# Two transformer layers on one core: three heads per attention slot, unpadded K, static tiles and hand-ordered streams

## Chip, core and metric

The kernel runs on one core of one Trainium2 chip. A core has a matrix engine (TensorE, PE in the profile, with its weight loads as PEld), a vector engine (DVE), a scalar engine that evaluates the exponential (ACT), GpSimd (POOL) and SyncE (SP), which here only issues transfers. Each engine works through its own queue in order; semaphores tie the queues together. Matmuls write to PSUM, a memory of eight banks of 512 fp32 columns on 128 partitions; ACT and DVE read from it.

The metric is device time in microseconds (us) of one execution. PEclk in the profile is the share of full TensorE speed that the clock throttle granted.

## What is computed

Two times the same pair of blocks: multi-head attention on the layer-normed x, added to x, then a ReLU MLP on the layer-normed x, added to x. Both layers use the same weights. S = 2048 tokens, D = 512, 32 heads of width 16, hidden width 1792; inputs and outputs are bfloat16.

```python
    def _A_ref(x, wqkv, wo):
        ...
        qkv = (lambda x, *d: x.transpose(*d))((x @ wqkv).reshape(B, S, 3, H, Dh), 2, 0, 3, 1, 4)
        q, k, v = qkv[0], qkv[1], qkv[2]
        scores = jnp.einsum("bhqd,bhkd->bhqk", q, k) * (Dh ** -0.5)
        p = _softmax(scores, axis=-1)
        o = jnp.einsum("bhqk,bhkd->bhqd", p, v)
        return (lambda x, *d: x.transpose(*d))(o, 0, 2, 1, 3).reshape(B, S, D) @ wo
    def _B_ref(x, w1, w2):
        h = jnp.einsum("bsd,df->bsf", x, w1)
        ...
        h = jnp.maximum(h, zero)
        return jnp.einsum("bsf,fd->bsd", h, w2)
    x = A_x
    x = x + _A_ref(_layernorm(x, axis=-1), A_wqkv, A_wo)
    x = x + _B_ref(_layernorm(x, axis=-1), B_w1, B_w2)
    x = x + _A_ref(_layernorm(x, axis=-1), A_wqkv, A_wo)
    x = x + _B_ref(_layernorm(x, axis=-1), B_w1, B_w2)
```

## The kernel before

**Tiling.** Tokens are cut into 16 tiles of 128 (for keys, for x and for the MLP) and 4 chunks of 512 queries. Heads go in 8 sets of four; head g of a set sits at partitions 32g to 32g + 15 of the padded Q and K (`wq_pad`, `wk_pad`, lines 81 to 97; half of each padded projection is zeros). One (chunk, set) pair is called a unit here: 32 units per layer, each over 16 key blocks.

**One key block of a unit.** `s_pair` (line 288, matmul at 293) computes transposed scores, 128 keys by 512 queries, of two heads into two banks, the heads on separate 32-row strips of the array. `e_pair` (301, the exponential at 303) takes the exponential of both at once, 128 x 1024, into SBUF. `pv_pair` (306, matmul at 310) multiplies by V, which carries a column of ones ahead of each head's 16 columns, so that row 0 of each head's strip of `pso` sums the exponentials. The pairs A and B (heads 0, 1 and 2, 3) take turns, each with two PSUM banks; `pso` has three buffers of one bank, cleared by DVE beforehand (319); the eighth bank, `ovl`, serves all other matmuls.

**Normalization** (`norm_item`, 322): copy of `pso`, a matmul with `esel` that spreads each sum over its strip (326), a copy (328), a reciprocal of 128 x 512 (329), a product (330).

**Filler work.** Q of the unit after next (`qchunk`, 204), output projection (`outproj_items`, 332), layer norms (`ln_stats_rstd` at 141 with a reciprocal square root by 13 Newton steps on DVE; `ln_apply` at 169 with four PE transposes a tile) and the MLP in halves of 256 tokens (`mlp_chunk_items`, 215) stand in two lists, `urgent` and `work`; `drain(1)` takes one entry after each key block. All their matmul groups share the `ovl` bank while attention runs. A scheduler of the tile framework settles the order on each engine's queue from the program order and priorities, so PE's order in the trace differs in places from the text.

**Stages.** Load and pad weights, layer norm of all 16 tiles, V for all, K for all (`vproj_all` 192, `kproj_all` 181); attention of layer one with the MLP of each finished chunk as filler; the remaining work with four PSUM buffers; V and K of layer two; attention of layer two; remaining work; stores.

**Queues of transfers.** SP: 16 loads of x, at the end 16 stores. POOL: wqkv. ACT: 32 small loads of `wo` rows (72), w1 and w2 (77, 79).

Of the kernel before, what the change touches and what calls it, by code (L numbers as in the profile page):

```python
# [10 lines left out]
BF16 = mybir.dt.bfloat16  # L11
ACTF = mybir.ActivationFunctionType
ALU = mybir.AluOpType

EPS = 1e-5


@with_exitstack
def kernel(
# [16 lines left out]
    H = 32  # L36
# [15 lines left out]
    identity_pool = ctx.enter_context(tc.tile_pool(name="identity_pool", bufs=1))  # L52

    ident = identity_pool.tile([P, P], BF16, name="ident")
    make_identity(nc, ident[:])

    x_tiles = []
    for tt in range(NTT):
        xt = persist.tile([P, D], BF16, name=f"x{tt}")
        nc.sync.dma_start(out=xt[:], in_=x_flat[tt * P : (tt + 1) * P, :])  # L60
        x_tiles.append(xt)

    wst_pool = tc.alloc_tile_pool(name="wst_pool", bufs=1)
    wqkv_st = wst_pool.tile([P, NDC, 3 * D], BF16, name="wqkv_st")
    nc.gpsimd.dma_start(out=wqkv_st[:], in_=A_wqkv[:, :].rearrange("(c p) f -> p c f", p=P))
    wo_pad = []
    for t in range(NT):
        wo_t = persist.tile([P, D], BF16, name=f"wo_pad{t}")
        nc.gpsimd.memset(wo_t[:], 0.0)
        for g in range(4):  # L70
            h = 4 * t + g
# [3 lines left out]
        wo_pad.append(wo_t)  # L75
    w1 = persist.tile([P, NDC, DFF], BF16, name="w1")
    nc.scalar.dma_start(out=w1[:], in_=B_w1[:, :].rearrange("(c p) f -> p c f", p=P))
    w2 = persist.tile([P, NF, D], BF16, name="w2")
    nc.scalar.dma_start(out=w2[:], in_=B_w2[:, :].rearrange("(c p) f -> p c f", p=P))

    wq_pad = []
    wk_pad = []
    for t in range(NT):
        wq_t = persist.tile([P, NDC, P], BF16, name=f"wq_pad{t}")
        wk_t = persist.tile([P, NDC, P], BF16, name=f"wk_pad{t}")
        nc.gpsimd.memset(wq_t[:], 0.0)
        nc.gpsimd.memset(wk_t[:], 0.0)
        for g in range(4):
# [43 lines left out]
    def gps():  # L132
        return cur_ps[0]
# [314 lines left out]
```

## Time and profile before

| | us |
|---|---|
| median of 3 runs | 2723.09 |
| lowest, highest run | 2709.48, 2730.97 |
| span of the profiled execution, first to last instruction | 2728.0 |
| PE busy | 2593.9 |
| ACT busy | 2049.6 |
| DVE busy | 840.6 |
| ACT idle before exponentials, waiting for scores | 447.9 |
| ACT idle before its table load, at the start | 106.0 |

The profile is of one execution; for that execution the span is the time there is, and it lies within the three runs, 4.9 us above their median. Busy time of an engine is the union of its instructions. A busy PE isn't PE at its best: at half clock the same matmul is busy for longer. A row of instructions reads: line, engine, operation, written tile <- read tiles, shapes, count, then busy time, mean ns of one, idle time of the engine just before them and what ended it. A timeline row reads: start, duration of the merged run of instructions, engine, line, operation, count. A matmul's modelled duration includes about 0.17 us in which the next one already streams.

### The profile page before, as it was taken

How to read it: one execution, taken by the hardware profiler on the slowest of the kernel's cores; microseconds unless marked ns; L12 is line 12 of the kernel's file. 1: busy time of each engine (PE TensorE's matmuls, PEld its weight loads, DVE VectorE, ACT ScalarE, POOL GpSimd, SP SyncE). 2: the span in 40 equal slices, each digit the busy share in tenths (PEclk: the TensorE clock that was granted, in tenths of full speed). 3: DMA queues.
4: the chain of work that ended last, by engine and by line, in shares of the span. 5: the costliest groups of instructions: out<-in, count | busy, mean ns of one | idle time of the engine just before them, and what ended most of it. 6: DMA issues, size and time to landing. Idle time of an engine off the chain costs nothing.

```text
span 2728.0 us, 27669 instructions
## 1 busy us (share of the span) xinstructions
PE 2593.9 (95%) x10752; PEld 645.9 (24%) x10752; DVE 840.6 (31%) x1842; ACT 2049.6 (75%) x2049; POOL 16.1 (1%) x52
## 2 busy tenths in 40 slices
PE   2999999999999999999859999999999999999996
PEld 1311112321222212232133111123212321123213
DVE  7411113321323214331274111143213331243215
ACT  0488886898758987589604888868987798869990
POOL 2000000000000000000000000000000000000000
PEclk9855556975558756595578555569755895569757
DMA  3000000000000000000000000000000000000000
GB/s 116 1 1 1 1 0 1 1 1 1 1 0 1 1 1 1 1 1 1 0 1 1 1 1 1 0 0 5 5 1 1 3 7 1 1 1 5 4 1 8
DMA packets 8371, 11.73 MB, mean 4 GB/s; under 512 B 1072, under 2 KB 7472, under 8 KB 8240
## 3 DMA queue, kind: packets, MB, share of 16 engines
q1 hardware_dynamic: 4608, 4.20, 0.5%
q10 hardware_dynamic: 3360, 4.20, 0.5%
q8 instruction: 84, 1.38, 0.2%
q0 software_dynamic: 272, 1.57, 0.1%
q14 instruction: 47, 0.39, 0.0%
HBM read 7.86 MB, written 2.10 MB: 4 GB/s over the span
## 4 chain that ended last, share of the span: by engine, by line
PE 85%; ACT 6%; DVE 6%; issue 2%; DMA 1%; ACTq 0%; SPq 0%
PE pss L293 33%; PE pso L310 32%; ACT expt L303 6%; PE ph L229 5%; PE pz L247 4%; PE poz L343 3%; PE pq L207 3%; PE pk L186 2%; PE pt L178 1%; PE pv L196 1%; PE pb L326 1%; DVE rs_t L162 1%; DVE rs_y L166 1%; DVE rs_t L160 1%; DVE rs_t L161 1%
## 5 line engine op out<-in xcount | busy, mean ns | idle before, releaser
L303 ACT ACTIVATE expt<-pss 128x1024 bf16<-128x1024 f32 x2048 | 2048.3, 1026 | 505.2 <-PE pss L293 447.9
L293 PE MATMUL pss<-qch,ktp 32*128 32x512 bf16 x4096 | 1140.9, 531 | 23.9 <-ACT expt L303 21.2
L310 PE MATMUL pso<-expt,vaug 128*17 128x512 bf16 x4096 | 1120.8, 527 | 0.9 <-ACT expt L303 0.9
L293 PEld LDWEIGHTS <-ktp 32*128 32x128 bf16 x4096 | 222.5, 96 | 834.2 <-issue 826.2
L310 PEld LDWEIGHTS <-vaug 128*17 128x17 bf16 x4096 | 194.3, 89 | 757.0 <-issue 747.1
L324 DVE CAST u<-pso 128x512 bf16<-128x512 f32 x64 | 44.1, 690 | 1048.1 <-PE pso L310 1048.1
L329 DVE RECIPROCAL pbs<-pbs 128x512 f32<-128x512 f32 x64 | 214.5, 3352 | 2.1
L229 PE MATMUL ph<-xn2T,w 128*128 128x256 bf16 x896 | 158.8, 302 | 0.9
L233 DVE TENSOR_SCALAR ht<-ph 128x256 bf16<-128x256 f32 x224 | 93.1, 418 | 210.3 <-PE ph L229 209.9
L178 PE MATMUL pt<-ident,xn 128*128 128x128 bf16 x256 | 56.9, 287 | 92.1 <-DVE xn L171 91.3
L247 PE MATMUL pz<-w,ht 128*128 128x512 bf16 x448 | 118.9, 382 | 0.6
L343 PE MATMUL poz<-wo_pad,ot 128*128 128x512 bf16 x256 | 103.1, 525 | 9.0 <-DVE x L348 4.7
L207 PE MATMUL pq<-xnT,wq_pad 128*128 128x512 bf16 x256 | 110.5, 511 | 1.2 <-DVE x L348 0.8
L229 PEld LDWEIGHTS <-w 128*128 128x128 bf16 x896 | 75.8, 105 | 74.8 <-issue 63.7
L303 ACT ACT_TABLE_LOAD x1 | 1.3, 1283 | 106.0 <-DVE qch L212 106.0
L212 DVE CAST qch<-pq 128x512 bf16<-128x512 f32 x64 | 44.1, 691 | 112.6 <-PE pq L207 111.8
L252 DVE TENSOR_TENSOR x<-x,pz 128x512 bf16<-128x512 bf16 x32 | 22.0, 687 | 147.6 <-PE pz L247 147.2
L348 DVE TENSOR_TENSOR x<-x,poz 128x512 bf16<-128x512 bf16 x32 | 22.0, 687 | 134.7 <-PE poz L343 134.7
L178 PEld LDWEIGHTS <-xn 128*128 128x128 bf16 x256 | 25.6, 112 | 156.6 <-DVE xn L171 100.2
L328 DVE COPY pbs<-pb 128x512 f32<-128x512 f32 x64 | 44.2, 691 | 40.6 <-PE pb L326 40.6
L186 PE MATMUL pk<-xnT,wk_pad 128*128 128x512 bf16 x256 | 55.6, 379 | 0.0
L179 DVE COPY xn2T<-pt 128x128 bf16<-128x128 bf16 x128 | 26.3, 222 | 91.1 <-PE pt L178 90.8
(41 smaller groups left out, 558.6 us busy)
## 6 DMA issues: line engine op xcount, KB each, us to landing
w<-in_B_w_dram ACTq DMA_DIRECT2D x2, 1792.0 KB, 10.9
x<-in_A_x_dram SPq DMA_DIRECT2D x16, 128.0 KB, 7.9
out_dram<-x SPq DMA_DIRECT2D x16, 128.0 KB, 1.7
wqkv_st<-in_A_wqkv_dram POOLq DMA_DIRECT2D x1, 1536.0 KB, 11.7
wo_pad<-in_A_wo_dram ACTq DMA_DIRECT2D x32, 16.0 KB, 1.7
```

The costliest lines, as they stand in the source:

```text
L178: nc.tensor.transpose(pt[:], xn[:, c * P : (c + 1) * P], ident[:])
L186: nc.tensor.matmul(pk[:], wk_pad[t][:, c, :], xnT[c][:, 512 * j : 512 * (j + 1)], start=(c == 0), stop=(c == NDC - 1),)
L207: nc.tensor.matmul(pq[:], wq_pad[t][:, c, :], xnT[c][:, qs * QS : (qs + 1) * QS], start=(c == 0), stop=(c == NDC - 1),)
L229: nc.tensor.matmul(ph[:], w1[:, c, ft * P : (ft + 1) * P], xn2T[c][:, c0 : c0 + HW], start=(c == 0), stop=(c == NDC - 1),)
L233: nc.vector.tensor_scalar(out=ht_half[ft][:], in0=ph[:], scalar1=0.0, scalar2=None, op0=ALU.max)
L247: nc.tensor.matmul(pz[:], ht_half[ft][:, ttl * P : (ttl + 1) * P], w2[:, ft, :], start=(ft == 0), stop=(ft == NF - 1),)
L293: nc.tensor.matmul(pss[:, QS * gi : QS * (gi + 1)], ktp[32 * g : 32 * g + 32, kb * P : (kb + 1) * P], qch[32 * g : 32 * g + 32, :], start= ...
L303: nc.scalar.activation(out=expt[:], in_=pss[:], func=ACTF.Exp, scale=SCALE)
L310: nc.tensor.matmul(pso[32 * g : 32 * g + VAW, :], vaug[kb][:, h, :], expt[:, QS * gi : QS * (gi + 1)], start=(kb == 0), stop=(kb == NKB - ...
L328: nc.vector.tensor_copy(out=pbs[:], in_=pb[:])
L329: nc.vector.reciprocal(out=pbs[:], in_=pbs[:])
L343: nc.tensor.matmul(pz[:], ot_all[t][:, ttl * P : (ttl + 1) * P], wo_pad[t][:], start=(t == 0), stop=(t == NT - 1),)
```

## The change

The function is rewritten. What it does, part by part:

- **Blocks and slots.** The unit of scheduling is a block (unit, key block, head). Three consecutive blocks form a slot: three score matmuls into one of two three-bank buffers `ps_s`, one exponential of 128 x 1536, and two slots later three value matmuls. Slots run on across key blocks and units; 2048 blocks of a layer make 683 slots. Four buffers hold exponentials.
- **PSUM.** Six banks for scores, one for the value sums (`ps_o`), one for filler work (`ps_f`). When attention isn't running (`wide`), filler work goes round seven banks.
- **Layouts.** K isn't padded: the projection's 128 columns hold eight heads of 16, four of them (even or odd) used per unit, and only Q's weights are padded with zeros, so that a contraction over a 32-row strip picks one head. There are 4 instead of 8 K projections per 512 tokens. V of head pairs is laid out with two columns of ones between them; a value matmul takes 32 columns, so the sum stands in row 16 or 15 of the strip. No clearing of the sums, no `esel` matmul.
- **Normalization.** Copy of `ps_o`, a stream shuffle on DVE that spreads the sum over its 32 partitions, the reciprocal in four parts of 128 columns, a product; after the copy, one such DVE instruction is issued per slot.
- **Reciprocal square root.** Bit-shift seed and 4 Newton steps of three instructions, per four tiles, where it was 13 steps of four.
- **Order.** The scheduler is off (`manual_schedule`): each engine runs in program order. All other work consists of pieces, mostly two matmuls each. `run_until` forces pieces that a slot needs; `run_some` paces the rest over the remaining slots of the chunk.
- **Start.** Layer norm, K and V of chunk 0 come first, then Q and the first slots; K and V of chunks 1 to 3 are made within the first unit, ahead of the key blocks that need them. K and V of layer two are made chunk by chunk as filler in layer one.
- **MLP** in chunks of 512 tokens instead of halves of 256.
- **Transfers.** On SP: four tiles of x, K's weights, the other tiles, 32 loads of `wo` rows, w1, w2; each output tile is stored when it is done. On ACT's queue: Q's and V's weights. Q's padded weights are built by POOL.

```diff
-    NT = H // 4
-    VAW = DH + 1
...
-    for t in range(NT):
-        wo_t = persist.tile([P, D], BF16, name=f"wo_pad{t}")
...
-            nc.scalar.dma_start(
-                out=wo_t[32 * g + 1 : 32 * g + 1 + DH, :], in_=A_wo[DH * h : DH * h + DH, :]
-            )
...
-    def ln_stats_rstd(tts):
...
-    def ln_apply(tt, xnT_dst, col0):
...
-    def kproj_all(xnT):
...
-    def vproj_all(xnT):
...
-    def mlp_chunk_items(qs, xnT_next, do_ln1next, work):
...
-    def mha_layer(xnT_cur, xnT_next, do_ln1next):
...
+    NT = 8
+    PW = 34
+    W = 3
+    NE = 4
+    ctx.enter_context(tc.manual_schedule())
...
+    ktp = [
+        [[sb([P, QS], BF16, f"ktp{l}_{T}_{j}") for j in range(NQS)] for T in range(4)]
+        for l in range(2)
+    ]
+    vaug = [[sb([P, H // 2, PW], BF16, f"vaug{l}_{kb}") for kb in range(NKB)] for l in range(2)]
+    ebuf = [sb([P, W, QS], BF16, f"e{n}") for n in range(NE)]
+    qbuf = [sb([P, QS], BF16, f"q{n}") for n in range(3)]
+    ubuf = [sb([P, QS], FP32, f"u{n}") for n in range(2)]
+    ps_s = [psum.tile([P, W, QS], FP32, name=f"ps_s{n}") for n in range(2)]
+    ps_o = psum.tile([P, QS], FP32, name="ps_o")
+    ps_f = psum.tile([P, QS], FP32, name="ps_f")
...
+    for tt in range(4):
+        nc.sync.dma_start(out=x_t[tt][:], in_=x_flat[tt * P : (tt + 1) * P, :])
+    nc.scalar.dma_start(out=wqkv[:, :, 0:D], in_=wq_src[:, :, 0:D])
+    nc.sync.dma_start(out=wqkv[:, :, D : 2 * D], in_=wq_src[:, :, D : 2 * D])
+    nc.scalar.dma_start(out=wqkv[:, :, 2 * D : 3 * D], in_=wq_src[:, :, 2 * D : 3 * D])
+    for tt in range(4, NTT):
+        nc.sync.dma_start(out=x_t[tt][:], in_=x_flat[tt * P : (tt + 1) * P, :])
...
+    for t in range(NT):
+        nc.gpsimd.memset(wq_pad[t][:], 0.0)
+    for kb in range(NKB):
+        nc.gpsimd.memset(vaug[0][kb][:, :, DH : DH + 2], 1.0)
+    for t in range(NT):
+        T, e = divmod(t, 2)
+        nc.gpsimd.tensor_copy(
+            out=wq_pad[t][:].rearrange("p c (g e d) -> p c g e d", g=4, e=2)[:, :, :, e, :],
+            in_=wqkv[:, :, T * P : (T + 1) * P].rearrange(
+                "p c (g e d) -> p c g e d", g=4, e=2
+            )[:, :, :, e, :],
+        )
+    for t in range(NT):
+        nc.gpsimd.memset(wo_pad[t][:], 0.0)
+        T, e = divmod(t, 2)
+        for g in range(4):
+            h = 8 * T + 2 * g + e
+            r0 = 32 * g + 16 * e
+            nc.sync.dma_start(out=wo_pad[t][r0 : r0 + DH, :], in_=A_wo[DH * h : DH * h + DH, :])
+    nc.sync.dma_start(out=w1[:], in_=B_w1[:, :].rearrange("(c p) f -> p c f", p=P))
+    nc.sync.dma_start(out=w2[:], in_=B_w2[:, :].rearrange("(c p) f -> p c f", p=P))
+    for kb in range(NKB - TPC):
+        nc.gpsimd.memset(vaug[1][kb][:, :, DH : DH + 2], 1.0)
+    def bank():
+        if not wide[0]:
+            return ps_f[:]
+        n = bank_no[0] % 7
+        bank_no[0] += 1
+        if n == 6:
+            return ps_f[:]
+        return ps_s[n // W][:, n % W, :]
+    def run_some(budget):
+        while budget > 0:
+            piece = next_piece()
+            if piece is None:
+                return
+            piece[1]()
+            budget -= piece[0]
+    def run_until(key):
+        while key not in done:
+            piece = next_piece()
+            assert piece is not None, key
+            piece[1]()
+    def ln_stats(j):
+        n = ln_no[0] % 2
+        ln_no[0] += 1
+        for i in range(TPC):
+            st = stats[i % 2]
+            nc.vector.bn_stats(out=st[:], in_=x_t[j * TPC + i][:])
+            nc.vector.bn_aggr(out=mv[n][:, i, :], in_=st[:])
+        a, y, t1 = va_[n], ya_[n], ta_[n]
+        nc.vector.tensor_scalar(
+            out=a[:], in0=mv[n][:, :, 1], scalar1=EPS, scalar2=None, op0=ALU.add
+        )
+        nc.vector.tensor_scalar(
+            out=t1[:].bitcast(I32), in0=a[:].bitcast(I32), scalar1=1, scalar2=None,
+            op0=ALU.logical_shift_right,
+        )
+        nc.vector.tensor_scalar(
+            out=y[:].bitcast(I32), in0=t1[:].bitcast(I32), scalar1=-1.0,
+            scalar2=float(RSQRT_SEED), op0=ALU.mult, op1=ALU.add,
+        )
+        for _ in range(4):
+            nc.vector.scalar_tensor_tensor(
+                out=t1[:], in0=y[:], scalar=-0.5, in1=y[:], op0=ALU.mult, op1=ALU.mult
+            )
+            nc.vector.tensor_mul(out=t1[:], in0=t1[:], in1=a[:])
+            nc.vector.scalar_tensor_tensor(
+                out=y[:], in0=t1[:], scalar=1.5, in1=y[:], op0=ALU.add, op1=ALU.mult
+            )
+        return n
+    def ln_groups(j, dst, key):
+        hold = {}
+        groups = []
+        def st():
+            hold["n"] = ln_stats(j)
+        for i in range(TPC):
+            def piece(i=i):
+                if i == 0:
+                    st()
+                n = hold["n"]
+                xn = xnbuf[i % 3]
+                nc.vector.tensor_scalar(
+                    out=xn[:], in0=x_t[j * TPC + i][:],
+                    scalar1=mv[n][:, i, 0:1], scalar2=ya_[n][:, i : i + 1],
+                    op0=ALU.subtract, op1=ALU.mult,
+                )
+                pt = bank().bitcast(BF16)
+                for c in range(NDC):
+                    nc.tensor.transpose(
+                        pt[:, c * P : (c + 1) * P], xn[:, c * P : (c + 1) * P], ident[:]
+                    )
+                nc.vector.tensor_copy(
+                    out=dst[:, :, i * P : (i + 1) * P],
+                    in_=pt[:, 0 : NDC * P].rearrange("p (c f) -> p c f", c=NDC),
+                )
+                if i == TPC - 1:
+                    done.add(key)
+            groups.append([(1.3, piece)])
+        return groups
+    def mm_group(mms, fin, per=2):
+        hold = {}
+        pieces = []
+        n = len(mms)
+        for a in range(0, n, per):
+            def piece(a=a):
+                if a == 0:
+                    hold["b"] = bank()
+                b = hold["b"]
+                for i in range(a, min(a + per, n)):
+                    lhsT, rhs = mms[i]
+                    nc.tensor.matmul(b, lhsT, rhs, start=(i == 0), stop=(i == n - 1))
+                if a + per >= n:
+                    fin(b)
+            pieces.append((min(per, n - a), piece))
+        return pieces
+    def k_group(l, T, j):
+        def fin(b):
+            nc.vector.tensor_copy(out=ktp[l][T][j][:], in_=b)
+            done.add(("k", l, T, j))
+        return mm_group(
+            [(wqkv[:, c, D + T * P : D + (T + 1) * P], xnT[j][:, c, :]) for c in range(NDC)], fin
+        )
...
+    def q_group(n, t, j):
+        def fin(b):
+            nc.vector.tensor_copy(out=qbuf[n % 3][:], in_=b)
+            done.add(("q", n))
+        return mm_group([(wq_pad[t][:, c, :], xnT[j][:, c, :]) for c in range(NDC)], fin)
+    def rest_of_chunk(l, j):
+        gs = [o_group(j, i) for i in range(TPC)]
+        gs += ln_groups(j, xn2T[:], ("ln2", l, j))
+        gs += [h_group(ft) for ft in range(NF)]
+        gs += [z_group(l, j, i) for i in range(TPC)]
+        if l == 0:
+            gs += before_attention(1, j)
+        return gs
+    def before_attention(l, j):
+        gs = ln_groups(j, xnT[j][:], ("ln", l, j))
+        gs.append(k_group(l, 0, j))
+        gs += [v_group(l, kb) for kb in range(j * TPC, (j + 1) * TPC)]
+        gs += [k_group(l, T, j) for T in range(1, 4)]
+        return gs
...
+    def norm_items(n, t):
+        u, r = ubuf[n % 2], rbuf[n % 2]
+        e = t % 2
+        lane = DH if e == 0 else DH - 1
+        def copy():
+            nc.vector.tensor_copy(out=u[:], in_=ps_o[:])
+        def shuf():
+            nc.vector.stream_shuffle(out=r[:], in_=u[:], mask=[lane] * 32)
+        def recip(a):
+            nc.vector.reciprocal(out=r[:, a : a + P], in_=r[:, a : a + P])
+        def mul():
+            nc.vector.tensor_mul(out=ot[t][:], in0=u[:], in1=r[:])
+        return copy, [shuf] + [lambda a=a: recip(a) for a in range(0, QS, P)] + [mul]
+    def emit_pv():
+        if not pend:
+            return
+        slot = pend[0]
+        n0 = slot["blocks"][0][0]
+        while slot["blocks"] and slot["blocks"][0][0] == n0:
+            n, kb, g, w = slot["blocks"].popleft()
+            l, j, t = units[n]
+            T, e = divmod(t, 2)
+            nc.tensor.matmul(
+                ps_o[32 * g : 32 * g + 32, :],
+                vaug[l][kb][:, 4 * T + g, 2 * e : 2 * e + 32],
+                slot["e"][:, w, :],
+                start=(kb == 0), stop=(kb == NKB - 1),
+                tile_position=(0, 32 * g), skip_group_check=True,
+            )
+            if kb == NKB - 1 and g == 3:
+                copy, rest = norm_items(n, t)
+                copy()
+                dve_q.extend(rest)
+                if t == NT - 1:
+                    dve_q.append(lambda l=l, j=j: work.extend(rest_of_chunk(l, j)))
+        if not slot["blocks"]:
+            pend.popleft()
...
+    def attention(l):
+        nonlocal slot_no
+        first = l * NQS * NT
+        blocks = deque(
+            (n, kb, g)
+            for n in range(first, first + NQS * NT)
+            for kb in range(NKB)
+            for g in range(4)
+        )
+        total = len(blocks) // (NQS * NT)
+        per_chunk = NT * NKB * 4 / W
+        while blocks:
+            now = [blocks.popleft() for _ in range(min(W, len(blocks)))]
+            for n, kb, g in now:
+                _, j, t = units[n]
+                if kb == 0 and g == 0:
+                    if n == first:
+                        urgent.append(q_group(n, t, j))
+                    if n + 1 < first + NQS * NT:
+                        _, jn, tn = units[n + 1]
+                        urgent.append(q_group(n + 1, tn, jn))
+                run_until(("q", n))
+                run_until(("k", l, t // 2, kb // TPC))
+            wide[0] = False
+            b = ps_s[slot_no % 2]
+            e = ebuf[slot_no % NE]
+            for w, (n, kb, g) in enumerate(now):
+                _, j, t = units[n]
+                kt = ktp[l][t // 2][kb // TPC]
+                kc = (kb % TPC) * P
+                nc.tensor.matmul(
+                    b[:, w, :],
+                    kt[32 * g : 32 * g + 32, kc : kc + P],
+                    qbuf[n % 3][32 * g : 32 * g + 32, :],
+                    start=True, stop=True, tile_position=(32 * g, 0),
+                )
+            m = len(now)
+            ex = nc.scalar.activation(
+                out=e[:, :m, :], in_=b[:, :m, :], func=ACTF.Exp, scale=SCALE
+            )
+            if last_exp[slot_no % NE] is not None:
+                tc.declare_no_dep(
+                    ex.ins, last_exp[slot_no % NE],
+                    reason="the matmuls that read the buffer between the two writes order them",
+                )
+            last_exp[slot_no % NE] = ex.ins
+            for n, kb, g in now:
+                run_until(("v", l, kb))
+            drain_pv(1)
+            pend.append(
+                {"e": e, "blocks": deque((n, kb, g, w) for w, (n, kb, g) in enumerate(now))}
+            )
+            if dve_q:
+                dve_q.popleft()()
+            slot_no += 1
+            rest = len(blocks) / W % per_chunk
+            todo = left(urgent) + left(work) + sum(c for c, _ in cur)
+            run_some(max(todo / max(rest - 6.0, 4.0), 0.01) if todo else 0)
+        drain_pv(0)
+        wide[0] = True
+        while dve_q:
+            dve_q.popleft()()
+        run_all()
...
+    for g in before_attention(0, 0):
+        urgent.append(g)
+    for j in range(1, NQS):
+        work.extend(before_attention(0, j))
+    attention(0)
+    attention(1)
```

`rest_of_chunk` calls `o_group`, `h_group` and `z_group`, which are `mm_group`s of 8, 4 and 14 matmuls whose last step on DVE adds to x, applies the ReLU, or adds to x and, in layer two, stores the tile. `v_group` is one of 4 matmuls per key block.

More of the change, by code (lines that the diff above doesn't have):

```diff
@@ L15 @@
 EPS = 1e-5
+RSQRT_SEED = 0x5F3759DF
 @with_exitstack
@@ new lines, in run_some, with run_all @@
+    def run_some(budget):
[10 more added lines that the diff above has]
+            piece[1]()
+    def run_all():
+        while True:
+            piece = next_piece()
+            if piece is None:
+                return
+            piece[1]()
```

396 lines of the change are left out of this document (88 added, 308 removed).

## The prediction

> **What bounds the kernel now.** I read the page's span and engine rows first, then the clock row, then the busy time by stretch, cut at the first and last exponential of each layer.
>
> ```profile
> span 2728.0 us, 27669 instructions
> PE 2593.9 (95%) x10752; PEld 645.9 (24%) x10752; DVE 840.6 (31%) x1842; ACT 2049.6 (75%) x2049; POOL 16.1 (1%) x52
> ACT  0488886898758987589604888868987798869990
> PEclk9855556975558756595578555569755895569757
> ...
> 0.00:107.33 107.33, 57.46 (x276) 27.12 (x276) 81.04 (x288) 1.28 (x1) 16.07 (x52) 1.00 0.22 74
> 107.33:1344.53 1237.20, 1224.38 (x4915) 278.08 (x4914) 322.90 (x606) 1025.71 (x1024) 0.00 (x0) 0.63 0.00 1
> 1344.53:1472.12 127.59, 92.22 (x459) 46.54 (x459) 94.81 (x282) 0.00 (x1) 0.00 (x0) 0.82 0.00 1
> 1472.12:2660.83 1188.71, 1175.33 (x4885) 270.63 (x4885) 302.85 (x543) 1022.60 (x1024) 0.00 (x0) 0.66 0.01 2
> 2660.83:2728.00 67.17, 44.54 (x219) 23.49 (x218) 38.99 (x124) 0.00 (x1) 0.00 (x0) 0.72 0.03 8
> ...
> 300.00:400.00 100.00, 100.00 (x368) 18.30 (x366) 13.52 (x13) 90.85 (x89) 0.00 (x0) 0.50 0.00 1
> 500.00:600.00 100.00, 97.55 (x519) 28.43 (x517) 34.99 (x47) 92.27 (x97) 0.00 (x0) 0.93 0.00 1
> ```
>
> A stretch row is: its time, then busy time and count of PE, weight loads, DVE, ACT, POOL, the granted clock, DMA. Three stretches have no exponential: 107 us of head, 128 between the layers, 67 of tail. The other 2426 us are attention, with PE at 99%, yet not at its best: between 300 and 400 PE is busy all the time at half clock. There only 368 − 4 x 89 = 12 matmuls are full-array ones; the others fill a quarter each. From 500 to 600, 519 − 4 x 97 = 131 full-array matmuls are mixed in and the clock is 0.93. So the granted clock follows how much of the array is filled, and the stretches without filler work are bound by a slow PE, those with it by ACT or by both in turn. The Trainium skill, "TensorE: Matmul & The Clock Gate", Part 1, has the full clock granted after some 3.4 us of sustained PE activity. If busy time is meant, the 300 to 400 row disagrees, 100% busy at 0.50; what the rule would make of the sum is rival D.
>
> Now the pitches inside attention.
>
> ```profile
> 251.21 0.61 PE L293 MATMUL pss<-qch,ktp 32*128 32x512 bf16 x2
> 251.75 0.60 PE L310 MATMUL pso<-expt,vaug 128*17 128x512 bf16 x2
> ...
> 493.31 0.39 PE L310 MATMUL pso<-expt,vaug 128*17 128x512 bf16 x3
> 493.63 0.39 PE L293 MATMUL pss<-qch,ktp 32*128 32x512 bf16 x2
> ...
> 496.11 1.04 PE L207 MATMUL pq<-xnT,wq_pad 128*128 128x512 bf16 x4
> 497.07 0.39 PE L310 MATMUL pso<-expt,vaug 128*17 128x512 bf16 x2
> ...
> 499.15 5.61 ACT L303 ACTIVATE expt<-pss 128x1024 bf16<-128x1024 f32 x6 [0.24 <-PE pss L293]
> ...
> L303 ACT ACTIVATE expt<-pss 128x1024 bf16<-128x1024 f32 x2048 | 2048.3, 1026 | 505.2 <-PE pss L293 447.9
> ```
>
> A pair of score matmuls, or of value matmuls, runs side by side and takes 0.54 us to the next group at half clock (251.21 to 251.75) and 0.32 at full (493.31 to 493.63). In that row three value matmuls, not two, fit in one 0.39 us group: a third tile rides along free. Four full matmuls take 0.96 us at full clock (496.11 to 497.07), of which 3 x 0.217 = 0.65 is between their starts (1.04 − 0.39); so one streams for 0.217 us, about twice that at half clock, and a change of shape costs about 0.10. Six exponentials take 5.61 us, one 1.026, so the pitch is (5.61 − 1.026)/5 = 0.917 us.
>
> **The change part by part.**
>
> *Slots of three.* 2 x 2048 blocks (32 units x 16 key blocks x 4 heads per layer) go in 683 slots per layer, 1366 in all, where there were 2048 exponentials. The price of a 1536-wide exponential isn't in the trace. Upper end: no fixed part, 1.5 x 0.917 = 1.376 us. For the fixed part the nearest rows are DVE evacuations of 512 and 256 columns:
>
> ```profile
> L329 DVE RECIPROCAL pbs<-pbs 128x512 f32<-128x512 f32 x64 | 214.5, 3352 | 2.1
> L233 DVE TENSOR_SCALAR ht<-ph 128x256 bf16<-128x256 f32 x224 | 93.1, 418 | 210.3 <-PE ph L229 209.9
> L190 DVE CAST ktp<-pk 128x512 bf16<-128x512 f32 x64 | 44.2, 691 | 11.0 <-PE pk L186 11.0
> L146 DVE BATCH_NORM_STATS2 stats<-x 128x6 f32<-128x512 bf16 x64 | 43.8, 687 | 1.7
> L330 DVE TENSOR_TENSOR ot<-u,pbs 128x512 bf16<-128x512 bf16 x64 | 43.7, 683 | 0.6
> L319 DVE MEMSET pso<- 128x512 f32 x64 | 31.0, 485 | 10.4 <-DVE u L324 8.9
> L171 DVE TENSOR_SCALAR xn<-x,mv_all,rstd_all 128x512 bf16<-128x512 bf16 x64 | 24.0, 406 | 0.4
> L162 DVE TENSOR_SCALAR rs_t<-rs_t 128x4 f32<-128x4 f32 (+2 forms) x130 | 22.1, 170 | 4.3
> ```
>
> 0.691 − 0.418 for 256 columns leaves 0.145 fixed. Taken over to ACT: (1.026 − 0.145) x 1.5 + 0.145 − (1.026 − 0.917) = 1.358. Twice that fixed part would give 1.285. I take 1.358, between the two: 1366 x 1.358 = 1855 us (1755 to 1880). The Trainium skill, "ScalarE: Activation LUTs", What ACT_TABLE_LOAD costs, gives 186 ns + 0.833 ns a column with 93 ns overlapped: an estimate of 1.372 a slot, which would make the sum below 19 us longer; for 1024 columns it says 1.039 for one alone, where the trace has 1.026.
>
> *PE beside it.* A slot needs one trio of score and one of value matmuls. Side by side as above: 0.64 us at full clock, 1.07 at half. Both are below 1.358, so plain attention is ACT-bound even at half clock. The pacing adds one piece of two full matmuls a slot while there is work: 2 x 0.217 + 0.10 = 0.53, together 1.17 at full clock; at half clock 1.07 + 0.87 + 0.10 = 2.03, too much. Work per chunk of layer 0, in pieces: 16 output projection, 4 layer norm, 28 hidden, 28 second MLP, 4 norm and 16 K/V for the next layer, 16 Q: 112 slots; of layer 1: 92. So 3 x 112 + 3 x 92 = 612 paced slots of 1366. Per 100 us they hold 100/1.358 x 2 = 147 full matmuls, more than the 131 of the 500 row: the clock should be full there, and half in the rest, where it does no harm.
>
> *The single filler bank.* A group's first matmul waits until DVE has emptied the one bank.
>
> ```profile
> 1352.30 0.39 PE L343 MATMUL poz<-wo_pad,ot 128*128 128x512 bf16 x1 [1.82 <-DVE ot L330]
> 1352.73 0.69 DVE L348 TENSOR_TENSOR x<-x,poz 128x512 bf16<-128x512 bf16 x1 [0.48 <-PE poz L343]
> 1353.47 3.33 PE L343 MATMUL poz<-wo_pad,ot 128*128 128x512 bf16 x8 [0.78 <-DVE x L348]
> ```
>
> From that matmul's end of streaming (1352.30 + 0.217) to the next is 0.95 us; the trios between cover 0.75. So 0.2 is exposed in at most every second slot: (1.17 + 1.37)/2 = 1.27, still under 1.358. I cost it at nothing; the cover is 0.09 a slot, and if it is gone see rival B.
>
> *Layer norm in the stream.* The first piece of a norm puts its transposes on PE's queue behind all DVE statistics: 4 x (0.687 + about 0.17 for its small follow-up) + 15 x 0.170 + 0.406 = 6.4 us, plus the 0.95 for the addition before, less 0.75 for the trios: PE, and the score trio queued behind, stand 6.6 us. ACT has about one slot in hand, so 5.6 us are lost, 9 times (6 in layer 0, 3 in layer 1): 50. The three later pieces each wait for their 0.406 us normalization behind a 0.69 copy: about 0.4 over, 27 times: 11. After such a hole the clock falls and some three slots run at 2.03: 2 us x 9 = 18. The chip's 13 Newton steps become 4; the old steps cost more, but the wait stays.
>
> *Unit ends.* The value sums have one bank instead of three, so the next unit's trio waits 0.95 for the copy. A slot has about 0.5 in hand: 0.45 x 64 = 29 us. A Q group alone in a plain stretch: two slots at 2.03, less the slack, 0.8 us; 36 units are plain (7 + 9 in layer 0, 8 + 12 in layer 1): 29.
>
> *Removed or moved at no cost.* The broadcast matmul, its copy and the 0.485 us clearing of each sum go; a shuffle takes their place (unseen; I take 0.69 by the copy row) and the reciprocal is cut in four, 0.84 each, one a slot. DVE has by these rows 64 x 6.1 for the norms, about 330 for the rest: a third of the span, not a bound. K without padding halves 256 matmuls and 64 copies. On SP, 4 + 12 loads of x with K's weights between, then 32 small loads and w1 and w2:
>
> ```profile
> 0.74 15.47 SPq L60 DMA_DIRECT2D x<-in_A_x_dram  x16
> x<-in_A_x_dram SPq DMA_DIRECT2D x16, 128.0 KB, 7.9
> out_dram<-x SPq DMA_DIRECT2D x16, 128.0 KB, 1.7
> w<-in_B_w_dram ACTq DMA_DIRECT2D x2, 1792.0 KB, 10.9
> ```
>
> At about 1 us an issue the last is out near 52 us and landed by 75; the MLP first needs it after 250. If SP ran four times slower, chunk 1 would wait. On POOL the padded K weights go and eight copies that build Q's come in, unseen there (between a 0.17 us small operation and a 0.69 us copy of DVE). POOL's whole old program is 16.07 us busy in the head row, and the first Q is due only near 25: nothing, or 10 more on the head if POOL were twice as slow.
>
> *Head, joint, tail.* Head: four x tiles at about 9, statistics 4, normalizing and transposing 4.5, 36 matmuls (K, V, Q of one chunk) about 12, two evacuations 1.9, table 1.3 (the one ACT instruction in the head row): 33 us for 107. In the first unit three more chunks are forced in ahead of their keys, each about 9 us: 27. Joint: last values 0.8, normalization 0.25 + 0.69 + 0.69 + 3.35 + 0.68 with waits 6.6, 32 projections (cold at first) 10, norm 11.4, 56 hidden matmuls 14.5, 56 second ones 12 + 1, norm 11.4, K/V 10, Q 2, first scores 0.6: 80 for 128. Tail: the same up to the second MLP product and 3 for the store (0.97 to issue by SP's row, 1.7 to land): 60 for 67.
>
> Sum: 33 + 27 + 1855 + 50 + 11 + 18 + 29 + 29 + 80 + 60 = 2192. The sum is made against the span of 2728.0, 4.9 above the median of the runs, 2723.09; I take those 5 off: 2187.
>
> **The rivals.** A, as summed: ACT sets the pace. Its own range is 2090 (exponential at its low end) to 2290 (stalls doubled).
>
> B: the filler bank and in-order waits set the paced slots at 1.7 us instead of 1.358 (PE trails, and each evacuation shows whole: 1.17 + 0.95/2 = 1.65). 612 x 0.34 = 208: 2395. For it: the 0.78 waits above. Against: the trios between groups.
>
> C: the clock stays at half while paced: 612 x (2.03 − 1.358) = 411, less the 18: 2580. For it: 300 to 400. Against: 500 to 600.
>
> D: the clock stays full all through, since three tiles fill three quarters where two filled half: 18 and 29 go, 2140. The 300 row speaks against, as far as two tiles go. By the clock rule of the Trainium skill cited above the time would be this one too.
>
> E, slower: score trios don't run as three; the third tile queues. It costs 0.217 a trio at full clock and 0.43 at half. Plain slots become 2 x (0.54 + 0.43) = 1.93 and paced ones 2 x (0.32 + 0.217) + 0.53 = 1.60: 754 x 1.93 + 612 x 1.60 = 2434, and with the other 337 us of the sum about 2770, up to 3570 where paced slots run at half clock too (1.93 + 0.87 + 0.10 = 2.90). It decides from a mean slot of (2728 − 337)/1366 = 1.75 us. Against: the row with x3; no row shows three score tiles.
>
> **How the numbers follow.** A 0.56, B 0.20, D 0.10, C 0.08, E 0.06. Likeliest 2187. Low to high 2090 to 2400 holds A, D and B, 0.86. Faster by over 1% (what a measurement here can tell from none) are A to D, 0.94; E is split 0.05 slower, 0.01 the same.
>
> **What would show it.** Right: exponentials 1.34 to 1.38 apart over long stretches; clock full where MLP matmuls run and half elsewhere; nine holes of about 6 us ended by the normalized tile; gaps of 33, 80 and 60 us without exponentials. Wrong: trios over 0.45 us at full clock (E), PE over 95% busy in paced stretches with ACT waiting for scores (B at a high clock, C at a low one).

## Result, and the profile after

The changed kernel takes 2257.75 us (median; 2256.56 to 2260.01), against 2722.32 for the kernel before in the same comparison: a ratio of 0.8334, 95% interval 0.8272 to 0.8396. The forecast was 2187, the range 2090 to 2400.

The page of the changed kernel (span, busy times, the 40 slices of ACT and clock), then its busy time by stretch, cut at the first and last exponential of each layer and after the first unit:

```profile
span 2255.5 us, 23128 instructions
PE 1837.2 (81%) x10112; PEld 511.4 (23%) x10112; DVE 697.0 (31%) x1312; ACT 1855.8 (82%) x1367; POOL 12.6 (1%) x58
ACT  1279997989989898989505999989997999989970
PEclk8775557986689757987576555689557975789558
...
0.00:37.97 37.97, 13.96 (x56) 5.68 (x57) 18.90 (x40) 1.29 (x2) 12.58 (x58) 1.00 0.64 207
37.97:131.06 93.09, 56.28 (x261) 16.69 (x259) 40.95 (x115) 29.70 (x22) 0.00 (x0) 0.71 0.00 1
131.06:1104.20 973.14, 818.52 (x4725) 223.94 (x4723) 303.61 (x557) 898.78 (x663) 0.00 (x0) 0.74 0.00 1
1104.20:1205.60 101.40, 63.73 (x218) 23.76 (x218) 44.06 (x101) 0.05 (x2) 0.00 (x0) 0.70 0.00 0
1205.60:2185.69 980.09, 841.13 (x4695) 224.37 (x4694) 260.21 (x438) 925.95 (x683) 0.00 (x0) 0.69 0.01 2
2185.69:2255.50 69.81, 43.54 (x162) 17.01 (x161) 29.26 (x61) 0.00 (x1) 0.00 (x0) 0.81 0.02 8
```

Attention went from 2426 us to 2046 (93 + 973 + 980), the head from 107 to 38, the joint between the layers from 128 to 101; the tail is 70 where it was 67. PE fell from 95% to 81% busy and ACT rose from 75% to 82%: the bound moved to ACT. Plain stretches look like this (timeline, start and duration):

```profile
259.41 24.50 ACT L448 ACTIVATE e<-ps_s 128x1536 bf16<-128x1536 f32 x18
259.59 0.61 PE L441 MATMUL ps_s<-q,ktp 32*128 32x512 bf16 x3 [0.62 <-ACT e L448]
260.93 0.61 PE L441 MATMUL ps_s<-q,ktp 32*128 32x512 bf16 x3 [0.19 <-ACT e L448]
```

Eighteen exponentials run without a gap, and three score matmuls take 0.61 us at half clock, as two did before; PE waits for ACT. The tenth percentile and the median of the time from one exponential's start to the next are both 1.330 us.

Attention's 2046 us are 230 more than the 1366 x 1.330 = 1817 us of the exponentials alone. In what follows a slot lasts from one exponential's start to the next; it is filled if PE runs filler work in it, and plain if not; a hole is a slot in which a norm's first piece makes ACT wait. The excess over 1.330, summed slot by slot from the trace, beside the terms of the forecast:

| | forecast | measured |
|---|---|---|
| head | 33 | 38 |
| first unit, excess | 27 | 65 |
| 1366 exponentials | 1855 | 1817 |
| nine norm holes | 50 | 67 |
| other slots: later norm pieces, recovery, unit ends, Q (11 + 18 + 29 + 29) | 87 | 98 |
| joint | 80 | 101 |
| tail | 60 | 70 |
| sum, span | 2192 | 2256 |

Of the 98, 65 lie in 121 filled slots at half clock, 14 in 521 filled slots at full clock (mean 1.356), 19 in 692 plain slots.

A norm hole, in timeline rows of the changed kernel, PE's weight loads left out:

```profile
376.69 0.39 PE L441 MATMUL ps_s<-q,ktp 32*128 32x512 bf16 x3
...
377.01 0.40 PE L389 MATMUL ps_o<-e,vaug 128*32 128x512 bf16 x3
377.40 0.94 DVE L372 RECIPROCAL r<-r 128x128 f32<-128x128 f32 x1
378.26 0.64 DVE L191 BATCH_NORM_STATS2 stats<-x 128x6 f32<-128x512 bf16 x1
...
384.50 0.41 DVE L230 TENSOR_SCALAR xn<-x,mv,ya 128x512 bf16<-128x512 bf16 x1
384.97 0.61 PE L237 MATMUL ps_f<-ident,xn 128*128 128x128 bf16 x4 [7.56 <-DVE xn L230]
385.51 0.61 PE L441 MATMUL ps_s<-q,ktp 32*128 32x512 bf16 x3
...
386.17 1.45 ACT L448 ACTIVATE e<-ps_s 128x1536 bf16<-128x1536 f32 x1 [7.37 <-PE ps_s L441]
```

The transposes stand at the head of PE's queue for 7.56 us, the score trio at 385.51 behind them, and ACT, which waits for that trio, idles 7.37. Transposes and trio run at half clock, 0.61 each, so ACT starts only 1.20 us after PE (384.97 to 386.17).

### The profile page after: what moved, and what is told of

Read it like the earlier page. It is cut to its first block, busy times and chain, and to the rows that moved or that the text cites. A ratio compares the mean times of both kernels' runs of the same rounds, so it can differ in the third digit from the quotient of the medians.

```text
span 2255.5 us, 23128 instructions
## 1 busy us (share of the span) xinstructions
PE 1837.2 (81%) x10112; PEld 511.4 (23%) x10112; DVE 697.0 (31%) x1312; ACT 1855.8 (82%) x1367; POOL 12.6 (1%) x58
## 4 chain that ended last, share of the span: by engine, by line
ACT 62%; PE 25%; DVE 11%; issue 1%; POOL 0%; SPq 0%; DMA 0%; ACTq 0%; POOLq 0%; DVEq 0%
ACT e L448 62%; PE ps_f L263 8%; PE ps_s L441 6%; PE ps_o L389 5%; PE ps_s L263 4%; DVE stats L191 2%; DVE u L366 1%; PE ps_f L237 1%; DVE ht L319 1%; DVE r L372 1%; DVE vaug L291 1%; DVE xn L230 1%; DVE ktp L272 1%; DVE q L304 1%; DVE mv L192 0%
## 5 line engine op out<-in xcount | busy, mean ns | idle before, releaser
L448 ACT ACTIVATE e<-ps_s 128x1536 bf16<-128x1536 f32 (+1 forms) x1366 | 1854.5, 1551 | 298.6 <-PE ps_s L441 295.2
L441 PE MATMUL ps_s<-q,ktp 32*128 32x512 bf16 x4096 | 697.2, 497 | 168.7 <-ACT e L448 150.3
L389 PE MATMUL ps_o<-e,vaug 128*32 128x512 bf16 x4096 | 719.9, 506 | 33.9 <-DVE u L366 33.0
L389 PEld LDWEIGHTS <-vaug 128*32 128x32 bf16 x4096 | 143.7, 97 | 492.9 <-issue 492.9
L372 DVE RECIPROCAL r<-r 128x128 f32<-128x128 f32 x256 | 221.9, 916 | 1.2
L263 PE MATMUL ps_f<-xn2T,w 128*128 128x512 bf16 x352 | 110.8, 400 | 9.1 <-DVE q L304 0.8
L319 DVE TENSOR_SCALAR ht<-ps_f 128x512 bf16<-128x512 f32 x88 | 60.9, 692 | 148.1 <-PE ps_f L263 148.1
L263 PE MATMUL ps_f<-w,ht 128*128 128x512 bf16 x350 | 104.5, 383 | 0.8
L263 PE MATMUL ps_f<-xnT,wq_pad 128*128 128x512 bf16 x248 | 100.9, 499 | 5.1 <-DVE x L331 1.6
L263 PE MATMUL ps_f<-wo_pad,ot 128*128 128x512 bf16 x208 | 69.2, 422 | 4.1 <-DVE ot L375 2.6
```

What stands on the lines that cost most here:

```text
L263: nc.tensor.matmul(b, lhsT, rhs, start=(i == 0), stop=(i == n - 1))
L319: nc.vector.tensor_scalar(out=ht[ft][:], in0=b, scalar1=0.0, scalar2=None, op0=ALU.max)
L372: nc.vector.reciprocal(out=r[:, a : a + P], in_=r[:, a : a + P])
L389: nc.tensor.matmul(ps_o[32 * g : 32 * g + 32, :], vaug[l][kb][:, 4 * T + g, 2 * e : 2 * e + 32], slot["e"][:, w, :], start=(kb == 0), stop ...
L441: nc.tensor.matmul(b[:, w, :], kt[32 * g : 32 * g + 32, kc : kc + P], qbuf[n % 3][32 * g : 32 * g + 32, :], start=True, stop=True, tile_po ...
L448: ex = nc.scalar.activation(out=e[:, :m, :], in_=b[:, :m, :], func=ACTF.Exp, scale=SCALE)
```

## Experiments

All are edits of the changed kernel. Ratios are to the kernel before, as timed on the same chip; times compare with the changed kernel's 2258. The kernel before has medians of 2711 to 2722 us in the four comparisons, so differences of some ten us between kernels of different comparisons rest on the traces, place by place, and not on the times.

One place moves without being touched, the joint. In the changed kernel it takes 101.40 us at a granted clock of 0.70 (the row 1104.20:1205.60 above); with the gap behind the norm's statistics, and with the pacing carried over, the same 218 matmuls take 6 us less:

```profile
1068.50:1164.23 95.73, 58.08 (x218) 22.63 (x218) 44.07 (x101) 0.01 (x2) 0.00 (x0) 0.77 0.00 0
1094.10:1188.91 94.81, 56.86 (x218) 22.33 (x218) 44.07 (x101) 0.00 (x1) 0.00 (x0) 0.79 0.00 0
```

Neither edit changes the work there. With the reciprocal whole the joint is 94.50 at 0.79. So 6 to 7 us of what these three runs gain or lose go with the clock in the joint; what raises it is open.

**Two heads a slot.**

```diff
-    W = 3
+    W = 2
...
-        n = bank_no[0] % 7
+        n = bank_no[0] % (2 * W + 1)
...
-        if n == 6:
+        if n == 2 * W:
```

> The changed kernel with slots of two heads (two-bank score buffers, exponentials of 128 x 1024, 2048 slots), all else kept. Theory: the gain in attention comes from the third tile riding along free, so that PE at half clock stays under the exponential. With two tiles a plain slot needs two groups of 0.54 us at half clock, 1.07, above the 0.903 that back-to-back exponentials of 1024 columns take; a paced slot needs 0.64 + 0.53 = 1.17 to 1.37 at full clock. 612 paced slots x 1.27 and 1436 plain ones x 1.08 make 2330 us where the changed kernel has 1860: about 2700 us in all, nearly the kernel before, and plain stretches with PE over 95% busy. Rival: the gain comes from layouts, static tiles and order. Then ACT still sets the pace: 2048 x 0.903 against 1366 x 1.330, 32 us more: about 2290.

Measured: 2730.47 us, ratio 1.0065 (1.0021 to 1.0108). Stretches of this run and a piece of its timeline:

```profile
0.00:35.41 35.41, 12.94 (x55) 5.52 (x56) 18.97 (x40) 1.28 (x1) 12.62 (x58) 1.00 0.63 196
35.41:1363.70 1328.29, 1217.11 (x4984) 279.23 (x4984) 341.87 (x672) 1035.38 (x1024) 0.00 (x0) 0.67 0.00 1
1363.70:1450.80 87.10, 53.85 (x217) 22.03 (x217) 44.08 (x101) 0.03 (x1) 0.00 (x0) 0.81 0.00 0
1450.80:2650.38 1199.58, 1142.67 (x4697) 258.25 (x4697) 256.81 (x438) 1032.07 (x1024) 0.00 (x0) 0.67 0.01 2
...
1300.00:1320.00 20.00, 20.00 (x76) 3.79 (x74) 1.01 (x2) 18.99 (x19) 0.00 (x0) 0.50 0.00 1
...
331.45 0.60 PE L441 MATMUL ps_s<-q,ktp 32*128 32x512 bf16 x2
331.99 0.61 PE L389 MATMUL ps_o<-e,vaug 128*32 128x512 bf16 x2
332.53 0.60 PE L441 MATMUL ps_s<-q,ktp 32*128 32x512 bf16 x2
```

Two tiles take the same 0.54 a group as three, so a slot is 1.08 and PE is busy for all of 1300 to 1320. The 1142 plain half-clock slots have a mean of 1.076; about 230 plain slots that still have the full clock are 0.906 apart, about what back-to-back exponentials take. The theory holds: without the third tile the rest of the change still shortens head and joint by 112 us together, and gives it back in attention, 2528 us where the kernel before has 2426.

**Two thirds of the exponential.** The third bank of a slot is left out of the exponential; its part of the buffers holds ones.

```diff
+    for e in ebuf:
+        nc.vector.memset(e[:], 1.0)
...
-                out=e[:, :m, :], in_=b[:, :m, :], func=ACTF.Exp, scale=SCALE
+                out=e[:, :2, :], in_=b[:, :2, :], func=ACTF.Exp, scale=SCALE
```

> The changed kernel with the exponential taken of only two of the three banks of each slot (the third part of the exponential buffer keeps constant ones, so a third of the softmax is left out); all matmuls stay. Theory (ACT sets the pace nearly everywhere): slots shrink until PE binds. Plain slots to 1.07 at half clock, or 0.90 if the denser matmuls pull the clock up; paced ones to 1.17 to 1.37. 612 x 1.27 + 754 x 0.90 to 1.07 plus about 400 of head, holes, joint and tail: 1860 to 1990 us. Rival (PE and its waits already set the pace of the paced slots and the exponential only that of the plain ones): plain slots shrink, paced ones stay at 1.36 or more: about 2000 to 2050. If ACT set no pace at all: 2257.

Measured: 1879.98 us, ratio 0.6927 (0.6875 to 0.6979). The clock row of its page:

```profile
PEclk9679998989989899898778999989998999999968
```

With slots packed closer the clock is full nearly everywhere, 0.92 on average. At the full clock 624 plain slots have a mean of 0.908, and 630 filled ones 1.283, which is PE's need with its waits for the filler bank, near the 1.27 of the prediction. So ACT's 1.330 covers that need by about 0.05 in the filled slots and by much more in the plain ones. ACT sets the pace; the rival by which paced slots would not shrink falls.

**A gap behind the norm's statistics.**

```diff
         def st():
             hold["n"] = ln_stats(j)
+        groups.append([(1.3, st)])
+        groups += [[(1.3, lambda: None)] for _ in range(5)]
...
-                if i == 0:
-                    st()
```

> The changed kernel with the statistics of a layer norm issued as a piece of their own and five empty pieces behind it, so that PE runs five more slots before the first transposes stand in its queue. Theory: the nine holes of 8.9 us are PE's in-order queue standing at transposes whose input DVE makes 7 us later; nothing needs the result yet. The holes go from 8.9 to under 2 us, 60 us off, and some of the half-clock slots behind them: 2190 to 2200. Rival: the norm is on the critical path or DVE is the bound there, so the wait comes back later: 2250 or more.

Measured: 2195.68 us, ratio 0.8088 (0.8040 to 0.8136), 62 less. The same place in its timeline:

```profile
371.35 17.66 ACT L449 ACTIVATE e<-ps_s 128x1536 bf16<-128x1536 f32 x13
...
383.44 5.58 ACT L449 ACTIVATE e<-ps_s 128x1536 bf16<-128x1536 f32 x4
...
388.60 0.61 PE L238 MATMUL ps_f<-ident,xn 128*128 128x128 bf16 x4 [1.06 <-DVE xn L231]
389.80 1.45 ACT L449 ACTIVATE e<-ps_s 128x1536 bf16<-128x1536 f32 x1 [0.78 <-PE ps_s L442]
```

The wait of 7.56 is 1.06 and ACT loses 0.78. It was a queue standing, not a bound on DVE. By place, the 67 us of the holes go, the other slots cost 11 more, and the joint is 6 shorter, as said above.

**Three tiles in turn outside attention.**

```diff
-        n = bank_no[0] % 7
+        n = bank_no[0] % 3
         bank_no[0] += 1
-        if n == 6:
+        if n == 2:
             return ps_f[:]
-        return ps_s[n // W][:, n % W, :]
+        return ps_s[n][:, 0, :]
```

> The changed kernel with filler groups outside attention going round three tiles (first bank of either score buffer and the filler bank) instead of the seven banks in order. Theory: consecutive groups in one three-bank buffer wait for DVE to empty the bank before, 0.78 us each, as dependencies are kept per tile and not per bank; these waits also keep the clock low between the layers. With three tiles in turn they go: the joint of 101 us falls to about 80, the tail of 70 to about 58, the head by 2: 2220. Rival: DVE's 0.69 us per evacuation is the bound there, and fewer banks change nothing or cost: 2257 or more.

Measured: 2220.48 us, ratio 0.8181 (0.8132 to 0.8230), 37 less. Hidden-layer matmuls between the layers, first the changed kernel, then this one:

```profile
1141.50 3.57 PE L263 MATMUL ps_s<-xn2T,w 128*128 128x512 bf16 x8 [0.78 <-DVE ht L319]
1145.85 1.86 PE L263 MATMUL ps_s<-xn2T,w 128*128 128x512 bf16 x4 [0.78 <-DVE ht L319]
1148.50 1.86 PE L263 MATMUL ps_s<-xn2T,w 128*128 128x512 bf16 x4 [0.78 <-DVE ht L319]
```

```profile
1135.09 1.67 PE L263 MATMUL ps_f<-xn2T,w 128*128 128x512 bf16 x4
1136.60 1.89 PE L263 MATMUL ps_s<-xn2T,w 128*128 128x512 bf16 x8
1138.32 1.03 PE L263 MATMUL ps_f<-xn2T,w 128*128 128x512 bf16 x4
```

The 0.78 waits and the half clock (1.86 for four, against 1.03) go together. In the changed kernel the next group in the same three-bank buffer waits for the evacuation of a different bank; the row of eight holds two groups with no wait between them, where the turn passes from one buffer to the other. The joint is 77 us, the tail 57, the head 34. Of the joint's 24, some 6 may be those that other runs win there untouched.

**Pacing carried over.** The unspent or overspent budget of a slot goes to the next; while output projection is left, one piece a slot.

```diff
...
-            run_some(max(todo / max(rest - 6.0, 4.0), 0.01) if todo else 0)
+            credit[0] += todo / max(rest - 6.0, 4.0)
+            if todo and o_left[0] > 0:
+                credit[0] = max(credit[0], 0.01)
+            credit[0] = run_some(credit[0]) if todo else 0.0
```

> The changed kernel with the pacing carried over from slot to slot, so that filler pieces are spread over the whole chunk instead of one in every slot until they are used up; the output projection keeps one piece a slot. Theory: in the changed kernel 121 slots with filler run at half clock and take 1.87 us instead of 1.33, 65 us in all, because the clock drops in the stretches without filler. Spread out, each window has filler, the clock stays full through chunks 1 to 3 of either layer, and 40 to 55 us go: 2200 to 2220. Rival: the clock falls between pieces all the same, or the added changes of shape eat it: 2250 or more.

Measured: 2222.20 us, ratio 0.8204 (0.8172 to 0.8236), 36 less: near the forecast time, but not by the forecast way. From 700 to 840 the clock is 0.92, where the changed kernel has 0.73 (first this run, then the changed kernel):

```profile
700.00:840.00 140.00, 111.22 (x721) 35.07 (x720) 45.04 (x84) 130.92 (x98) 0.00 (x0) 0.92 0.00 1
```

```profile
700.00:840.00 140.00, 117.45 (x682) 32.09 (x679) 43.69 (x82) 128.91 (x96) 0.00 (x0) 0.73 0.00 1
```

Yet the excess of filled half-clock slots is 73 us where it was 65. What shrank is the nine holes, from 67 to 49, since a norm's first piece no longer follows in the very next slot, the joint by 6.5, and plain slots by 10. My theory of the clock fell here: a full clock in stretches that ACT paces buys no more than the 10 of the plain slots.

**K of later head sets made later.**

```diff
+    for j in range(NQS):
+        gs = before_attention(0, j)
+        (urgent if j == 0 else work).extend(gs[:-3])
+    for T in range(1, 4):
+        work.extend(k_group(0, T, j) for j in range(NQS))
```

> The changed kernel with K of head sets 2 to 4 of all chunks made after the norms, first K and V of all chunks, instead of chunk by chunk. Theory: the two gaps of 20 us in the first unit each hold 12 K matmuls with three waits for the filler bank, about 5.5 us, that no slot needs before the third unit; behind them comes the forced norm. Without them the gaps fall to 15, and the head loses 5 us: 15 us off, 2243. Rival: the work has to be done anyway within the first chunk and only moves: 2257.

Measured: 2231.78 us, ratio 0.8238 (0.8208 to 0.8268), 26 less where 15 were expected. The first 20 us gap is 15, the second falls apart into two in a row, of 8 and 6; the head is 34.5, the first unit's excess 53 instead of 65. That is 16 us, as expected. The other 10 are the joint, 91.37 us at a clock of 0.79, which this edit touches only in where the turn of the banks starts; the runs above win 6 to 7 of that with no such touch.

**The reciprocal whole.** One instruction of 512 columns for four of 128.

```diff
-            nc.vector.reciprocal(out=r[:, a : a + P], in_=r[:, a : a + P])
+            nc.vector.reciprocal(out=r[:], in_=r[:])
```

> The changed kernel with the reciprocal of a unit in one instruction of 512 columns instead of four of 128. Theory of the cut: an evacuation of the filler bank queued behind it on DVE waits up to 3.4 us instead of 0.9, PE stands at the next group and ACT loses 1 to 2 us in each of some 29 paced units: 2290 to 2310. Rival: the slots' slack covers it, or what is lost is won back by three DVE instructions fewer: 2257, within 10.

Measured: 2293.77 us, ratio 0.8461 (0.8423 to 0.8499), 36 more. In its timeline:

```profile
420.76 3.35 DVE L372 RECIPROCAL r<-r 128x512 f32<-128x512 f32 x1
...
424.03 0.63 DVE L319 TENSOR_SCALAR ht<-ps_f 128x512 bf16<-128x512 f32 x1
...
424.71 0.59 PE L263 MATMUL ps_f<-xn2T,w 128*128 128x512 bf16 x2 [1.93 <-DVE ht L319]
425.67 1.45 ACT L448 ACTIVATE e<-ps_s 128x1536 bf16<-128x1536 f32 x1 [1.57 <-PE ps_s L441]
```

The evacuation waits behind the reciprocal, PE stands 1.93 us for its bank, ACT 1.57. The filled slots cost 33 us more than in the changed kernel and the holes 11 more. One thing is mixed in: a unit's DVE work now ends three slots earlier, so a chunk's remaining work starts earlier too. The joint, 7 shorter, hides a part: without it the loss is 43.

**Together.** First all four gains, then three without the carried-over pacing, then all four with the next tile's normalization ahead of this tile's copy.

```diff
-                nc.vector.tensor_scalar(
-                    out=xn[:], in0=x_t[j * TPC + i][:],
...
-                )
+                if i == 0:
+                    norm(0)
...
+                if i + 1 < TPC:
+                    norm(i + 1)
```

> The changed kernel with the norm gap, the three-tile rotation, the carried-over pacing and the later K together. If the four costs are separate places, their gains add up: 62 + 37 (both measured) + about 45 + 15 = 159 off 2258: 2100. If they share slack, 2130 to 2160.

> The norm gap, the three-tile rotation and the later K together, with the changed kernel's own pacing. In the carried-over pacing alone the filled half-clock slots cost as much as before (73 us against 65) and the holes shrank (53 against 67), so its 35 us seem to come from holes that the norm gap removes anyway. Theory: with the gap in place the pacing adds next to nothing; the three gains 62 + 37 + 26 add up: 2133, within 8 of the version with all four (2128). Rival: the pacing has a gain of its own by the clock: 2150 to 2165.

> The version with all four, with the normalization of the next tile put on DVE ahead of the copy of this one. Theory: in each norm PE waits three times for the 0.4 us normalization behind a copy, 0.3 to 0.5 us each, in all 16 norms: 48 x 0.3 to 0.4 less what slots hide: 8 to 15 us off, 2112 to 2120. Rival: the slots at half clock are bound by PE's own work there, and only the joint, the tail and the first unit gain: 2122 to 2126.

Measured: 2127.57 (ratio 0.7859, 0.7828 to 0.7890); 2138.15 (0.7915, 0.7859 to 0.7971); 2121.02 (0.7849, 0.7780 to 0.7919). Gap, rotation and later K alone should add up to 62 + 37 + 26 = 125, that is 2133, and give 120. The sum fits better than its parts: the joint is 25 shorter where the three alone make 40, and the other slots cost 7 more where they make 18. On top of the three the pacing gives 11, a little more than the 8 of the theory and far from the rival, of the 36 that it gives alone: the rest is mostly the holes, which the gap takes too, and the joint.

The normalization ahead gives 7, between its theory and its rival by the time. By place it is the rival: head, first unit, joint (77 to 71) and tail are 12 us shorter together, and the rest of attention is 6 longer. The last version beats both kernels.

## Why the prediction was right

The mechanism held in its main steps: ACT sets the pace, by three tiles a group. Of the signs named, the clock and what ended the nine holes came as said; the exponentials are 1.330 apart, just under the 1.34 to 1.38 named, the holes cost 7.4 us instead of about 6, and the stretches without exponentials take 38, 101 and 70 us instead of 33, 80 and 60.

*Slots of three*: the third tile rides free, in score groups too, where no row had shown it (rival E is out; two heads a slot give the old time back). *PE beside it*: plain attention is ACT-bound at half clock, 616 such slots at a mean of 1.355; paced stretches have the full clock (521 filled slots, 1.356). So B and C are out, and D too, since plain stretches stay at 0.50. That the clock follows how much of the array is filled, as the prediction inferred from two rows, is not shown by that (see the last section). *The single filler bank* costs next to nothing while the reciprocal is cut; the whole one shows how thin that cover is. The reciprocal's cut, costed at nothing, is worth 36 us or so.

The sizes, with the step of each:

- The exponential, taken at 1.358 between 1.285 and 1.376, is 1.330: 38 us too much. About half is the pitch of 1024 columns, taken as 0.917 where back-to-back ones are 0.904 apart. The other half is the fixed part of one exponential, taken over from DVE as 0.145: at the measured 0.832 ns a column, 1.026 leaves 0.174, and in the prediction's formula a larger fixed part makes the slot shorter.
- "ACT has about one slot in hand" in the norm step was wrong: PE stood 7.56, as against 6.6, because one part of a reciprocal (0.94) was ahead of the statistics on DVE. ACT lost nearly all of it, 7.4 a hole instead of 5.6, since the transposes and the trio at half clock take 1.20 more before it can start.
- The first unit was mis-sized as much, 65 for 27. I counted a forced norm's wait and few matmuls behind it; its two longest gaps have 20 us each. They also hold 12 K matmuls with three waits for the filler bank, and every forced tile costs 0.84 of wait for its normalization. Of the 38 us missed, the later K shows 12; the forced norms' serial chain of DVE and PE is the likely rest. The normalization ahead takes 3 us of it; the chain as a whole was not tried.
- The joint's and tail's 80 and 60 took the seven banks as independent. They are not: three banks form one tile, and dependencies go by tile. With three tiles in turn they measure 77 and 57, near the two sums.
- The recovery of the clock after a hole, 18 us, was seen as a cost of the clock. The filled half-clock slots are mostly those of the norm pieces (16 us, for 11 + 18 in the forecast) and of Q (34 for 29); making the clock full elsewhere leaves the cost of such slots where it was. The unit ends, 29 in the forecast, are in the 19 of the plain slots.

The errors partly cancel: 38 us too much for the exponential against 102 too little elsewhere. So part of the number's nearness is luck.

## What to carry to other kernels

Count what a group of small tiles costs as a group, at the clock that the stretch will really have: a third tile that rides free can move the bound from PE to ACT, and then PE's clock matters only in slots that PE fills. In hand-ordered streams, put the producer's instructions several slots ahead of the consumer's in another engine's queue, not just ahead. And check what a dependency is kept for: buffers that are separate banks but one tile wait for each other.

## What was not expected of the hardware

The exponential's pitch is 0.904 us for 1024 columns (two heads a slot) and 1.330 for 1536: 0.832 ns a column and only 0.05 us fixed, though one instruction of 1536 columns lasts 1.45 us where it is short and 1.55 on average. The slope agrees with the 0.833 ns of the Trainium skill, "ScalarE: Activation LUTs", What ACT_TABLE_LOAD costs; its fixed part of 186 − 93 ns is larger than the pitch shows, so the estimate of 1.372 worked out from it was high.

The clock doesn't follow busy time alone. With two tiles a group PE is 100% busy for 20 us at 0.50. Three tiles alone don't hold the full clock either. In the run with two thirds of the exponential, these two rows lie in one stretch of 40 plain slots:

```profile
900.00:920.00 20.00, 15.35 (x129) 5.96 (x126) 5.87 (x10) 20.00 (x22) 0.00 (x0) 1.00 0.00 1
921.00:938.00 17.00, 17.00 (x96) 3.29 (x93) 3.71 (x5) 16.05 (x16) 0.00 (x0) 0.50 0.00 1
```

Behind the last filler work PE keeps the full clock for 20 us, 77% busy; then it has half the clock for 17 us, 100% busy. The run's other stretch of 40 plain slots goes the same way; its other long ones end after 15 to 20 slots, before the clock has fallen. The Trainium skill, "TensorE: Matmul & The Clock Gate", Part 1, speaks of sustained activity; a busy PE alone is not what counts as such here, and these runs don't show what does.
